# Moving the residual loads and the whole output stores from GpSimd's DMA queue to SyncE's

## The chip, the cores and the metric

The kernel runs on one core of one Trainium2 chip. The metric is device time in microseconds (us) of one execution, the median of several runs; lower is better. Engines are named as in the profile: PE is TensorE's matmuls, PEld its weight loads, DVE is VectorE, ACT is ScalarE, POOL is GpSimd, SP is SyncE. A "q" behind an engine's name (SPq, POOLq) means its instruction queue: instructions that set up, wait, branch or issue a DMA and do no arithmetic. Each queue takes its instructions strictly in order, so an instruction that waits holds all that stand behind it on the same engine.

## The reference

One layer over 2048 tokens of width 512, in bf16, is the sum of three terms: the residual x, a sliding-window attention of the normalized x, and a gated MLP of it that mixes tokens.

```python
def _A_ref(x, wqkv, wo):            # 32 heads of 16, window of 256 tokens
    ...
    p = _softmax(scores, axis=-1)
    o = jnp.einsum('bhqk,bhkd->bhqd', p, v)
    return (lambda x, *d: x.transpose(*d))(o, 0, 2, 1, 3).reshape(B, S, D) @ wo

def _B_ref(x, w_in, w_sp, b_sp, w_out):
    z = _gelu(jnp.einsum('bsd,df->bsf', x, w_in))
    z1 = z[..., :Fh].copy()
    z2 = _layernorm(z[..., Fh:], axis=-1)
    g = jnp.einsum('ts,bsf->btf', w_sp, z2) + b_sp[None, :, None]
    return jnp.einsum('bsf,fd->bsd', z1 * g, w_out)
x = A_x
xn = _layernorm(x, axis=-1)
return x + _A_ref(xn, A_wqkv, A_wo) + _B_ref(xn, B_w_in, B_w_sp, B_b_sp, B_w_out)
```

## The kernel before

**First stage (to about 84 us).** x is loaded, normalized and transposed into xnT; `z_half` (L280) makes both halves of z with a GELU; part of the q, k and v projections (`qkv_unit`, L111 and L129) is mixed in. POOL computes the reciprocal square roots (L238).

**Second stage (from about 84 us to the end).** The tokens are 16 tiles of 128, numbered t, and for attention 8 pairs of tiles, numbered J. The order of the work on PE is written out by hand in the string `ORDER`: S is a group of attention scores, m a mask, p the product with v, n a normalization, and the letters q, g and f with a number are so many matmuls of the projections, of the token mixing and of the output. The units that matter here:

- `g_work(t, j)` (L426 to L448): 16 matmuls of w_sp's transposed tile wspT(t) with z2, for half j of the columns; DVE then multiplies with z1 into u (L439). After the second half SP issues the transpose uT(t) of u by DMA (L446), and right behind it the load of wspT(t+2), also a DMA transpose (L414). There are two buffers of wspT.
- `f_work(t, c0)` (L462 to L487): 6 matmuls with uT(t) and 4 with the attention's transposed result, into one bank; DVE adds the residual tile xo(t) in place (L481), and the sum is stored from xo(t) to the output, out(t) (L487). Tile 15 is done in two halves of 256 columns, whose stores, out(15a) and out(15b), go out from SP and ACT.
- `load_xo(t)` (L452): the residual tile, 128 KB, into one of four buffers. Tiles 0 and 1 are asked for ahead of the second stage, and tile t+2 at the head of `f_work(t)`.
- `load_half(J)` (L403): two DMAs on SP (L406, L408) that copy parts of v into vh for pair J.
- `check_sums` (L628), called between DVE's addition of tile 13 and out(13): DVE checks the attention sums in three instructions, and SP sends the result `low` as one row by DMA (`row`, L639). At the end DVE reduces that row to a flag (L823, L826), all five engines load the flag (L829) and branch on it (L834): a second version of the attention runs if a sum was out of bounds, and is skipped here.

Behind the branch stands the end of the program (under L859 in the profile): SP waits for every DMA's and every engine's counter, each engine drains, and all meet at a barrier which POOL gathers and releases; then POOL clears the counters and all meet once more.

No scheduler moves instructions: each engine runs what the program records for it, in the order of recording. DMA completions are counted on eight counters for DMAs issued by SP and ACT, in turn, and on eight others for those of POOL.

Of the kernel before, what the change touches and what calls it, by code (L numbers as in the profile page):

```python
# [8 lines left out]
P = 128  # L9
# [6 lines left out]
D = 512  # L16
# [37 lines left out]
def kernel(  # L54
# [12 lines left out]
    nc = tc.nc  # L67
    x2 = A_x.flatten_outer_dims()
# [74 lines left out]
    with ExitStack() as actx:  # L143
# [20 lines left out]
        for half in range(2):  # L164
            for k, eng in ((0, nc.sync), (1, nc.scalar)):
# [3 lines left out]
                    out=w_in_sb[:, :, f0 : f0 + HALF], in_=w_in_v[:, :, f0 : f0 + HALF]  # L169
# [5 lines left out]
        with nc.allow_non_contiguous_dma(reason="tiny bias gather"):  # L175
# [3 lines left out]
            out=w_out_sb[:, 0:5, :], in_=B_w_out[0:640, :].rearrange("(c p) n -> p c n", p=P)  # L179
# [5 lines left out]
        for _ in range(WARM):  # L185
# [7 lines left out]
            out=hmask[:],  # L193
            in_=ident[:].rearrange("p (s e d) -> p e s d", s=4, e=2),
# [16 lines left out]
        for m, off in ((maskY, 0), (maskD, -PAD)):  # L211
            nc.gpsimd.memset(m[:], 1.0)
            nc.gpsimd.affine_select(
                out=m[:, 0:PAD], in_=m[:, 0:PAD], pattern=[[-1, PAD]],
# [3 lines left out]
                out=m[:, PAD:P], in_=m[:, PAD:P], pattern=[[1, PAD]],  # L218
# [231 lines left out]
    xos = {}  # L450

    def load_xo(t):  # L452
        xos[t] = cp.tile([P, D], BF, name="xo", bufs=4)
        nc.gpsimd.dma_start(out=xos[t][:], in_=x2[t * P : (t + 1) * P, :])

    for t in range(2):
        load_xo(t)

    def f_cols(t):
        return D // 2 if t == NB - 1 else D  # L460

    def f_work(t, c0):  # L462
        if c0 == 0 and t + 2 < NB:
            load_xo(t + 2)
        xo = xos[t]
        w = f_cols(t)
        fo = ps_x.tile([P, 512], F32, name="fo", tag="f")
        for ch in range(NFC):
            nc.tensor.matmul(  # L469
                fo[:, 0:w], lhsT=uTs[t][:, ch, :], rhs=w_out_sb[:, ch, c0 : c0 + w],  # L470
                start=(ch == 0), stop=False,
            )
            yield
        q0 = (1 - t % 2) * P
        for c in range(NC):
            nc.tensor.matmul(  # L476
                fo[:, 0:w], lhsT=oTs[t // 2][:, c, q0 : q0 + P], rhs=wo_sb[:, c, c0 : c0 + w],
                start=False, stop=(c == NC - 1),
            )
            yield  # L480
        nc.vector.tensor_tensor(  # L481
            out=xo[:, c0 : c0 + w], in0=fo[:, 0:w], in1=xo[:, c0 : c0 + w], op=ALU.add
        )
        if t == NB - 3:
            check_sums()
        eng = (nc.sync if c0 == 0 else nc.scalar) if w < D else nc.gpsimd
        eng.dma_start(out=out2[t * P : (t + 1) * P, c0 : c0 + w], in_=xo[:, c0 : c0 + w])  # L487

    E = {}
# [138 lines left out]
    def check_sums():  # L628
        assert not (later or units)
        r = r_all[:].rearrange("p a b -> p (a b)")  # L630
        ok = ep.tile([P, 512], BF, name="ok", tag="E")
        low = ep.tile([P, 1], F32, name="low", tag="E")
        nc.vector.tensor_scalar(out=ok[:], in0=r, scalar1=R_LOW, scalar2=None, op0=ALU.is_ge)
        nc.vector.scalar_tensor_tensor(
            out=ok[:], in0=r, scalar=R_HIGH, in1=ok[:], op0=ALU.is_le, op1=ALU.mult
        )
        nc.vector.tensor_reduce(out=low[:], in_=ok[:], axis=mybir.AxisListType.X, op=ALU.min)
        row = ep.tile([P, P], F32, name="row", tag="E")
        nc.sync.dma_start(out=row[0:1, :], in_=low[:])  # L639
        rows.append(row)  # L640


    def attention_with_maximum(gctx):
# [153 lines left out]
        "q": [(4, q_work(b, i)) for b, i in qkv_list],  # L797
        "g": [(NB, g_work(t, j)) for t in range(NB) for j in range(2)],
        "f": [(NFC + NC, f_work(t, c0)) for t in range(NB) for c0 in range(0, D, f_cols(t))],
    }  # L800
    left = 0
    for step in ORDER.split():
# [21 lines left out]
        out=low[0:1, :], in_=rows[0][0:1, :], axis=mybir.AxisListType.X, op=ALU.min  # L824
    )
    nc.vector.tensor_scalar(  # L826
        out=flag[0:1, :], in0=low[0:1, :], scalar1=0.5, scalar2=None, op0=ALU.is_lt
# [36 lines left out]
```

## Time and profile before

| what | value |
|---|---|
| runs of the kernel | 261.93, 262.01, 262.93 us, median 262.01 |
| span of the profiled execution, first to last instruction | 259.3 us |
| median less that span (what lies around it) | 2.7 us |
| PE busy | 250.8 us, 97% of the span |
| DVE, ACT, POOL busy | 205.2, 196.3, 36.9 us (79%, 76%, 14%) |
| granted TensorE clock | 0.999 |
| DMA | 25.86 MB, mean 100 GB/s |
| loads of xo by POOL | 16, of 128 KB, 2.4 us from issue to landing in the median |
| whole stores by POOL | 15, of 128 KB, 2.6 us in the same count |

The profiled execution has no other time of its own than its span; the three runs are other executions. The profile's page gives busy time by engine, a strip of 40 slices, the DMA queues, the chain of work that ended last, and the costliest groups of instructions. Views of the trace behind it list who waited for whom, the instructions of one line of the kernel (with the shortest, median and longest duration in nanoseconds), and each engine's instructions in order of time.

### The profile page before, as it was taken

How to read it: one execution, taken by the hardware profiler on the slowest of the kernel's cores; microseconds unless marked ns; L12 is line 12 of the kernel's file. 1: busy time of each engine (PE TensorE's matmuls, PEld its weight loads, DVE VectorE, ACT ScalarE, POOL GpSimd, SP SyncE). 2: the span in 40 equal slices, each digit the busy share in tenths (PEclk: the TensorE clock that was granted, in tenths of full speed). 3: DMA queues.
4: the chain of work that ended last, by engine and by line, in shares of the span. 5: the costliest groups of instructions: out<-in, count | busy, mean ns of one | idle time of the engine just before them, and what ended most of it. 6: DMA issues, size and time to landing. Idle time of an engine off the chain costs nothing.

```text
span 259.3 us, 8817 instructions
## 1 busy us (share of the span) xinstructions
PE 250.8 (97%) x3857; PEld 142.4 (55%) x3877; DVE 205.2 (79%) x425; ACT 196.3 (76%) x236; POOL 36.9 (14%) x80
## 2 busy tenths in 40 slices
PE   8999999999999999999999999999999999999991
PEld 2665555555555455655664565455565565646651
DVE  4796997874656888598888788989899978858781
ACT  2777546446456899999999999999989986888300
POOL 4120312111011530101010110111011021010100
PEclk9999999999999999999999999999999999999999
DMA  7984021027300206585174537846056925751321
GB/s 220 370 227 161 0 43 40 0 52 124 70 0 4 63 19 142 134 155 116 44 100 123 134 64 140 130 111 132 27 89 153 147 76 118 119 125 44 72 53 48
DMA packets 61707, 25.86 MB, mean 100 GB/s; under 512 B 53648, under 2 KB 59200, under 8 KB 61664
## 3 DMA queue, kind: packets, MB, share of 16 engines
q1 hardware_dynamic: 58688, 20.15, 38.1%
q0 software_dynamic: 1488, 4.07, 4.8%
q10 hardware_dynamic: 1488, 1.03, 1.4%
q8 instruction: 31, 0.51, 0.8%
q14 instruction: 12, 0.10, 0.2%
HBM read 8.41 MB, written 2.10 MB: 41 GB/s over the span
## 4 chain that ended last, share of the span: by engine, by line
PE 95%; DVE 1%; DMA 1%; issue 1%; POOL 0%
PE gf L433 31%; PE zp L280 14%; PE S L558 10%; PE o L519 9%; PE fo L469 8%; PE pj_o L111 7%; PE fo L476 6%; PE pj_f L111 4%; PE pj_f L129 3%; PE pj_o L129 2%; DMA xt<-in_A_x_dram 1%; PE tp L270 1%; DVE stats L228 1%; POOL rs L238 0%; DVE xo L481 0%
## 5 line engine op out<-in xcount | busy, mean ns | idle before, releaser
L608 ACT ACTIVATE E<-S 128x1024 bf16<-128x1024 f32 (+1 forms) x128 | 117.5, 1007 | 8.3 <-PE S L558 8.0
L433 PE MATMUL gf<-z2n,wspT 128*128 128x344 bf16 x512 | 83.3, 310 | 0.0
L433 PEld LDWEIGHTS <-wspT 128*128 128x128 bf16 x512 | 46.6, 98 | 28.6 <-issue 5.5
L280 PE MATMUL zp<-w_in_sb,xnT 128*128 128x344 bf16 x256 | 41.8, 309 | 0.0
L611 DVE TENSOR_TENSOR E<-E,maskY 128x2048 bf16<-128x2048 bf16 (+2 forms) x36 | 37.9, 1058 | 2.5 <-ACT E L608 2.4
L280 PEld LDWEIGHTS <-xnT 128*128 128x128 bf16 x256 | 24.8, 98 | 15.2
L583 ACT ACTIVATE ED<-S 128x1024 bf16<-128x1024 f32 x32 | 31.0, 1023 | 2.3 <-PE S L558 2.3
L558 PE MATMUL S<-qpad,kT 32*64 32x128 bf16 (+1 forms) x1008 | 32.6, 246 | 0.2
L526 DVE STREAM_TRANSPOSE ot<-o 128x512 f32<-128x512 f32 x32 | 22.3, 716 | 7.9 <-PE o L519 7.8
L487 POOL DMA_DIRECT2D out_dram<-xo x15 | 8.2, 546 | 120.7 <-DVE xo L481 111.5
L558 PEld LDWEIGHTS <-kT 32*64 32x64 bf16 (+1 forms) x1008 | 12.2, 98 | 22.3 <-issue 21.3
L469 PE MATMUL fo<-w_out_sb,uT 128*128 128x512 bf16 (+1 forms) x90 | 23.3, 366 | 0.9 <-issue 0.5
L439 DVE SCALAR_TENSOR_TENSOR u<-gf,b_all,z 128x344 bf16<-128x344 f32 x32 | 18.2, 568 | 7.3 <-PE gf L433 6.8
L519 PE MATMUL o<-E,v_y 128*32 128x128 bf16 (+1 forms) x736 | 23.1, 239 | 0.0
L238 POOL TENSOR_TENSOR rs<-ve,mhalf 128x2 f32<-128x2 f32 (+1 forms) x17 | 11.7, 690 | 69.4 <-DVE ve L235 69.4
L519 PE MATMUL o<-ED,vh 128*32 128x64 bf16 x960 | 21.1, 193 | 0.0
L287 ACT ACTIVATE z<-zp 128x688 bf16<-128x688 f32 x16 | 11.9, 744 | 11.0 <-PE zp L280 11.0
L111 PE MATMUL pj_o<-xnT,wqkv 128*128 128x512 bf16 x77 | 20.1, 379 | 0.2
L287 ACT ACTIVATE z2n<-zp 128x688 bf16<-128x688 f32 x16 | 11.9, 744 | 10.3 <-PE zp L280 10.3
L111 PEld LDWEIGHTS <-wqkv 128*128 128x128 bf16 x128 | 12.5, 98 | 12.6
L611 DVE TENSOR_TENSOR ED<-ED,maskC 128x2048 bf16<-128x2048 bf16 x16 | 19.4, 1210 | 0.0
L122 DVE TENSOR_SCALAR qpad<-qt,hmask 128x512 bf16<-128x512 bf16 x32 | 9.7, 346 | 11.8 <-ACT qt L120 11.8
(70 smaller groups left out, 264.8 us busy)
## 6 DMA issues: line engine op xcount, KB each, us to landing
vh<-v_y SPq DMA_DIRECT2D x15, 140.0 KB, 3.5
xo<-in_A_x_dram POOLq DMA_DIRECT2D x16, 128.0 KB, 2.4
out_dram<-xo POOLq DMA_DIRECT2D x15, 128.0 KB, 2.6
xt<-in_A_x_dram SPq DMA_DIRECT2D x3, 512.0 KB, 10.3
wqkv<-in_A_wqkv_dram SPq DMA_DIRECT2D x1, 1536.0 KB, 10.9
w_in_sb<-in_B_w_in_dram ACTq DMA_DIRECT2D x2, 344.0 KB, 5.7
w_in_sb<-in_B_w_in_dram SPq DMA_DIRECT2D x2, 344.0 KB, 6.2
w_out_sb<-in_B_w_out_dram SPq DMA_DIRECT2D x1, 640.0 KB, 6.0
```

Of the source, the lines that this page charges most:

```text
L111: nc.tensor.matmul(pt[:], lhsT=wqkv[:, c, w0 : w0 + P], rhs=xnT[:, c, t0 : t0 + 512], start=(c == 0), stop=(c == NC - 1),)
L280: nc.tensor.matmul(zp[:, j, 0:HALF], lhsT=xnT[:, c, PAD + n * P : PAD + (n + 1) * P], rhs=w_in_sb[:, c, f0 : f0 + HALF], start=(c == 0), s ...
L287: nc.scalar.activation(out=dst.rearrange("p (j f) -> p j f", j=2), in_=zp[:, :, 0:HALF], func=ACT.Gelu_apprx_tanh,)
L433: nc.tensor.matmul(gf[:, 0:HALF], lhsT=wspT[t][:, c, :], rhs=z2n[:, c, j * HALF : (j + 1) * HALF], start=(c == 0), stop=(c == NB - 1),)
L439: nc.vector.scalar_tensor_tensor(out=u[:, j * HALF : (j + 1) * HALF], in0=gf[:, 0:HALF], scalar=b_all[:, t : t + 1], in1=z1[:, t, j * HALF ...
L469: nc.tensor.matmul(fo[:, 0:w], lhsT=uTs[t][:, ch, :], rhs=w_out_sb[:, ch, c0 : c0 + w], start=(ch == 0), stop=False,)
L519: nc.tensor.matmul(o[32 * s : 32 * s + 32, c0 + r0 : c0 + r0 + n], lhsT=v[:, m, h * VW : h * VW + 32], rhs=rhs(s), start=(i == 0), stop=(i ...
L526: nc.vector.transpose(out=ot[:].rearrange("p b j -> p (b j)"), in_=o[:])
L558: nc.tensor.matmul(out, lhsT=kT[32 * s : 32 * s + 32, g, k0 : k0 + nk], rhs=qpad[J // 2][32 * s : 32 * s + 32, g, :, qs - q00 : qs - q00 + ...
L583: nc.scalar.activation(out=Ed[:, 16 * i : 16 * i + 16, :], in_=S[i][:].rearrange("p b (x q) -> p (b x) q", q=PAD), func=ACT.Exp, scale=SM_ ...
L608: nc.scalar.activation(out=o, in_=w, func=ACT.Exp, scale=SM_SCALE)
L611: nc.vector.tensor_tensor(out=out, in0=in0, in1=mask.unsqueeze(1).to_broadcast([P, in0.shape[1], in0.shape[2]]), op=ALU.mult,)
```

## The change

All loads of the residual (L454) and the fifteen whole stores of the output (L487) are issued by SP in place of POOL. The two half stores of tile 15 stay on SP and ACT.

```diff
     def load_xo(t):
         xos[t] = cp.tile([P, D], BF, name="xo", bufs=4)
-        nc.gpsimd.dma_start(out=xos[t][:], in_=x2[t * P : (t + 1) * P, :])
+        nc.sync.dma_start(out=xos[t][:], in_=x2[t * P : (t + 1) * P, :])
...
         if t == NB - 3:
             check_sums()
-        eng = (nc.sync if c0 == 0 else nc.scalar) if w < D else nc.gpsimd
+        eng = nc.scalar if c0 > 0 else nc.sync
         eng.dma_start(out=out2[t * P : (t + 1) * P, c0 : c0 + w], in_=xo[:, c0 : c0 + w])
```

The built programs show the same instructions in the same order on PE, DVE and ACT. POOL loses 31 instructions that issue a DMA and is left with memsets in the second stage; SP gains the 31. On SP they stand where the program records them: the load xo(t+2) at the head of `f_work(t)` and the store out(t) at its end, among the transposes, the loads of wspT and the copies into vh. The end of SP's work reads, in the order of the changed program: uT(14), xo(14), out(12), uT(15), xo(15), row, out(13), out(14), out(15a), load of the flag. At the end of the program SP's list of waits is eight long instead of twelve, since POOL's eight DMA counters (two in a wait) are gone.

## The prediction

> **What bounds the kernel now.** First I read the page's busy times and its chain of work that ended last.
>
> ```profile
> span 259.3 us, 8817 instructions
> PE 250.8 (97%) x3857; PEld 142.4 (55%) x3877; DVE 205.2 (79%) x425; ACT 196.3 (76%) x236; POOL 36.9 (14%) x80
> PE 95%; DVE 1%; DMA 1%; issue 1%; POOL 0%
> ```
>
> PE is the bound: busy for 97% of the span, 95% of the chain. In PE's instructions in order of time, the gaps from 88 to 254 us add up to under 1 us. So what the change touches can win nothing inside the second stage; it can only lose there, by delivering something late. What it could win lies where PE is idle: before about 6 us, where POOL issues no DMA, and after PE's last matmul, which ends at 253.9.
>
> Next, who waited for whom, for SP and POOL (columns: total wait in us, times, longest):
>
> ```profile
> SPq L446 <- DVE u L439: 95.0, 16, 11.5
> POOL out_dram L487 <- DVE xo L481: 111.5, 14, 14.9
> ```
>
> Both queues mostly wait for DVE: POOL to store xo, SP to transpose u. The 31 moved issues have room on SP if no wait holds what stands behind it.
>
> Third, the end. These are POOL's and SP's own instructions under L859, from 255.85 to 258.5 us and then from 258.5 on (count, shortest/median/longest in ns, first and last start):
>
> ```profile
> L859 POOLq DRAIN  x1: 2597/2597/2597, 255.9 to 255.9; - x1
> ```
>
> ```profile
> L859 SPq EVENT_SEMAPHORE  x12: 28/28/28, 256.1 to 256.8; - x12
> L859 SPq DRAIN  x2: 7/10/13, 256.8 to 256.9; - x2
> ```
>
> ```profile
> L859 POOLq EVENT_SEMAPHORE  x4: 17/17/17, 258.5 to 259.2; - x4
> L859 POOLq DRAIN  x2: 44/76/107, 258.7 to 259.0; - x2
> ```
>
> POOL stands in one DRAIN from 255.9 to 255.9 + 2.6 = 258.5. SP, the slowest of the others, is through its waits at 256.9. Only at 258.5 does POOL gather the barrier, and 0.8 us later the span ends. So the last wait of this program is POOL's DRAIN, 1.6 us longer than anything else needs. It is no wait for data: POOL's last store was issued at 252.91 and landed 2.0 us later, at 254.9, before the DRAIN began.
>
> **The change, part by part.** (xo(t), out(t), uT(t), wspT(t) are the DMAs of tile t; vh(J) the two of pair J.)
>
> *POOL without DMAs.* Its 31 issues of 0.55 us (17 us) go. They lay in POOL's waits and on no path of PE: 0.
>
> *The DRAIN.* What does it cost on a POOL that issued no DMA? The trace before can't show that. Its other POOL DRAINs bound it: 0.04 and 0.11 us right after the long one, 0.18 us at 0.4 us behind four memsets. The upper end is the 2.6 us itself. I take 0.1 us, the nearest rows: in the long one POOL had no arithmetic left (its last memset is at 242.1), and unfinished business of its DMA queue is what sets it apart from the short ones. The Trainium skill (VectorE: DVE Perf Modes, The DRAIN you can't avoid) gives the boilerplate DRAINs of all five engines as constant at about 12 ns. The 7 to 13 ns of SP's agree, the 2597 ns does not, so by that page it isn't boilerplate alone; with 12 ns in place of 0.1 us the sum would be the same, because SP then comes last.
>
> *What is late next.* SP. Its twelve waits take 0.7 us from 256.1 to 256.8, 0.06 us each. The changed program has eight, as POOL's DMA counters are gone: 4 x 0.06 = 0.25 us less. SP's last drain moves from 256.9 to 256.65, POOL gathers at 256.7 in place of 258.5: a gain of **1.8 us**. If the DRAIN stays at 2.6 us, the gain is 0.
>
> *31 more issues on SP, and who stands behind their waits.* An issue of a plain DMA on SP takes 0.39 (64 KB) to 0.58 us (128 KB): about 31 x 0.5 = 15 us, beside 95 us of waits on u alone. The danger is a store that waits for DVE's addition with a transpose behind it. I set the time at which POOL issued each store (its tile summed by then) against SP's issue of the next transpose: out(0) 122.2 before uT(4) 130.5; out(3) 151.26 before uT(6) 153.72; out(7) 187.73 before uT(9) 190.25; out(8) 198.12 before uT(10) 200.58; out(10) 211.1 before uT(11) 215.4; out(11) 231.6 before uT(14) 238.7; out(12) 241.6 before uT(15) 247.15. The smallest margin is 2.46 us, more than four issues of 0.58. Stores hold no transpose up: 0. The Trainium skill (DMA: Bandwidth & Descriptors, Anatomy of one DMA — SWDGE (gpsimd) path) says that any wait for a semaphore is held on the issuing sequencer. That speaks against the change, and by these margins it costs nothing until the end.
>
> *Loads of wspT.* They are needed soon. Issue plus time to landing, against PE's first matmul on it: wspT(2) 101.25 against 102.45, wspT(3) 109.2 against 110.6, wspT(13) 216.69 + 4.4 = 221.1 against 222.27, wspT(14) 223.54 + 5.8 = 229.3 against 230.2. Ahead of the first two SP gains only xo(0) and xo(1), at 84 to 86 us, where it is idle. Ahead of wspT(13), out(10) (ready at 211.1) now pushes the pair vh(7) from 205.1 to about 211.7; vh took 3.0 to 5.4 us to land, so it may be in flight until 217. wspT took 4.3 to 6.9 us: the cost is between 0 and 6.9 - 5.6 = 1.3 us. I take 0, the row itself (4.4 us), since vh is all but landed by then. Ahead of wspT(14) nothing is added.
>
> *xo(15).* It was issued on POOL at 242.23. On SP it stands behind uT(15), which waits for u: that is issued at 247.15 for 1.76 us, so xo(15) goes at 248.97. DVE needs it at 252.80, and may take it up to 253.5 without delaying the last addition (253.96 less 0.42 us of work). It must land within 4.5 us. xo took 2.4 us in the median on POOL's queue, SP's first 128 KB loads 4.1, the longest xo or store 5.0. Cost between 0 and 0.5 us; I take 0, by the 2.4 us.
>
> *Stores at the end.* out(13) was issued at 250.53. On SP it stands behind row, which waits for DVE's check until 252.10 and takes 0.52. Then out(13) at 252.7, out(14) at 253.3, out(15a) at 253.9, done at 254.3, ahead of the load of the flag at 254.76. A landing of 1.9 to 2.6 us brings out(15a) home by 255.8 to 256.5; SP's waits for the counters run from 256.1 to 256.6. Cost 0 to 0.3; I take 0.
>
> **Sum.** 259.3 - 1.8 = 257.5 us of span. Around the span lie 262.01 - 259.3 = 2.7 us, which I leave as they are: **260.2 us**, 0.7% below the median. A difference under 0.5% (1.3 us) can't be told from none.
>
> **The rivals.**
>
> *1. The DRAIN stays.* If its 2.6 us come from something else (being POOL's first DRAIN after a long program), the barrier is gathered at 258.5 as before: 262.0 us. For it: nothing shows what POOL does in it, and POOL's DMAs had landed. Against it: three short DRAINs on the same engine. By the Trainium skill (DMA: Bandwidth & Descriptors, Issuing engines are not separate DMA queues) issuing from several engines only saves sequencer time; by that the result would be the same 262.0. The rows here have the 17 us of issue time in waits, which agrees, but that rule is silent on the DRAIN. Chance 0.20.
>
> *2. Slower: xo(15) comes late.* One mechanism: on one queue, xo(15) stands behind a transpose that waits for the last u. Every us that it takes beyond 4.5 to land delays the last additions, the flag and the branch by as much. From 4.5 + 1.8 = 6.3 us on, the gain at the DRAIN is eaten. With the 6.9 us of the slowest wspT it is 260.2 + 2.4 = 262.6; with the 10.3 us of the x loads of the first stage, issued into full queues, 266.0. For it: the queue was slow whenever much stood in it. Against it: in the slice from 238 to 248 us the DMA engines are busy 0.21 of the time, and ahead of xo(15) stands only uT(15), which landed after 3.0 us. Chance 0.09.
>
> *3. Part is given back.* The DRAIN shrinks, but wspT(13) stalls PE by up to 1.3 us, or the last stores keep SP: 260.8 to 261.8 us. Chance 0.07.
>
> That the change doesn't do what it says is ruled out by the changed program: POOL issues no DMA there.
>
> **How the numbers follow.** The forecast has 0.64. Faster by over 0.5% means below 260.7: nearly all of the forecast, 0.62. Slower by over 0.5% means above 263.3: most of rival 2, with what I have not seen, 0.09. The rest is the same: rival 1, rival 3 and the edges, 0.29. Around the forecast the bounds reach from 0.6 us below (POOL's steps behind the barrier, two DRAINs of 0.107 and 0.044 us and a clearing of counters of 0.178, are 0.3 us that may shorten with fewer counters, and the runs of before differ by 0.1 us at the least and more) to 0.5 above. To leave out no more than 2 in 10 the range must take in rivals 3 and 1: 259.6 to 262.4 us. The forecast's own range is 259.6 to 260.7.
>
> **What would show it.** Right: POOL's DRAIN at 255.9 falls to about 0.1 us, its first EVENT_SEMAPHORE under L859 stands at 256.7, SP has eight waits there, and PE's last matmul still ends at 253.9. Step by step: SP's uT issues stand at the times above; PE shows no idle time before gf at 222.3; xo(15) lands before 252.8; DVE's last addition begins at 253.96. Wrong: a DRAIN of 2 us or more without DMAs (rival 1); the additions of tile 15 released by a DMA (rival 2); new gaps on PE before gf or fo (rival 3).

## The result, and the profile after

The changed kernel takes 259.92 us in the median of 6 runs (259.21 to 260.23), the kernel before, run beside it, 261.97 (6 runs, 261.42 to 262.93). The ratio is 0.9914, with a 95% interval of 0.9893 to 0.9935: faster by 0.9%. The forecast was 260.2.

The page after, first the same three lines as were shown of before:

```profile
span 258.2 us, 8833 instructions
PE 252.7 (98%) x3877; PEld 142.4 (55%) x3877; DVE 205.1 (79%) x425; ACT 196.5 (76%) x236; POOL 20.2 (8%) x49
PE 96%; DVE 1%; DMA 1%; issue 0%; POOL 0%
```

PE bounds the kernel as before. (Its busy time can't be compared here: the page after has 20 matmul records more.) POOL's 17 us of DMA issues are gone (36.9 to 20.2 us). The end of the program shows where the time went. POOL's and SP's instructions under L859 up to 257.4 us, and POOL's from there on (count, shortest/median/longest in ns, first and last start):

```profile
L859 POOLq DRAIN  x1: 41/41/41, 256.3 to 256.3; - x1
```

```profile
L859 SPq EVENT_SEMAPHORE  x8: 28/28/28, 256.9 to 257.3; - x8
L859 SPq DRAIN  x1: 13/13/13, 257.4 to 257.4; - x1
```

```profile
L859 POOLq EVENT_SEMAPHORE  x4: 17/17/17, 257.5 to 258.1; - x4
L859 POOLq DRAIN  x2: 34/58/82, 257.6 to 257.9; - x2
L859 POOLq EVENT_SEMAPHORE_RANGE_CLEAR  x1: 135/135/135, 257.7 to 257.7; - x1
```

The DRAIN of 2597 ns is one of 41 ns. POOL now waits for SP: SP's eight waits end at 257.4, POOL gathers at 257.46. To compare two executions here, count from the load of the flag (L829), since PE's work ended 0.75 us later in this one. Before, it began at 254.76, the gather came 3.77 us later and the end 4.55 us later; after, it began at 255.52, with the gather 1.94 and the end 2.64 us later. The end has become shorter by 1.91 us.

SP's queue from 84 us on (total wait, times, longest) shows that the 31 issues went into its waits:

```profile
SPq L446 <- DVE u L439: 60.5, 16, 8.6
SPq L487 <- DVE xo L481: 18.6, 6, 6.7
```

SP waits for u 60.5 us in place of 95.0, still 16 times: each transpose of u still waits for its data and not for a store.

### The profile page after: what moved, and what is told of

Same layout as the page of the kernel before. It is cut to its first block, busy times and chain, and to the rows that moved or that the text cites. A ratio compares the mean times of both kernels' runs of the same rounds, so it can differ in the third digit from the quotient of the medians.

```text
span 258.2 us, 8833 instructions
## 1 busy us (share of the span) xinstructions
PE 252.7 (98%) x3877; PEld 142.4 (55%) x3877; DVE 205.1 (79%) x425; ACT 196.5 (76%) x236; POOL 20.2 (8%) x49
## 4 chain that ended last, share of the span: by engine, by line
PE 96%; DVE 1%; DMA 1%; issue 0%; POOL 0%
PE gf L433 31%; PE zp L280 15%; PE S L558 11%; PE o L519 9%; PE fo L469 9%; PE pj_o L111 7%; PE fo L476 6%; PE pj_f L111 4%; PE pj_f L129 3%; PE pj_o L129 2%; DMA xt<-in_A_x_dram 1%; PE tp L270 1%; DVE stats L228 1%; POOL rs L238 0%; DVE xo L481 0%
## 5 line engine op out<-in xcount | busy, mean ns | idle before, releaser
L469 PE MATMUL fo<-w_out_sb,uT 128*128 128x512 bf16 (+1 forms) x102 | 24.6, 368 | 0.0
L476 PE MATMUL fo<-wo_sb,oT 128*128 128x512 bf16 (+1 forms) x68 | 17.7, 368 | 0.0
L519 PEld LDWEIGHTS <-v_y 128*32 128x32 bf16 x736 | 15.2, 97 | 4.0 <-issue 3.6
```

Source lines behind the costliest of these rows:

```text
L469: nc.tensor.matmul(fo[:, 0:w], lhsT=uTs[t][:, ch, :], rhs=w_out_sb[:, ch, c0 : c0 + w], start=(ch == 0), stop=False,)
L476: nc.tensor.matmul(fo[:, 0:w], lhsT=oTs[t // 2][:, c, q0 : q0 + P], rhs=wo_sb[:, c, c0 : c0 + w], start=False, stop=(c == NC - 1),)
L519: nc.tensor.matmul(o[32 * s : 32 * s + 32, c0 + r0 : c0 + r0 + n], lhsT=v[:, m, h * VW : h * VW + 32], rhs=rhs(s), start=(i == 0), stop=(i ...
```

## The experiments

**The kernel before, again.** No edit.

> The kernel before, unchanged: 262.0 us as before, and a span for each of its runs, which the first runs of before did not have. The median fell by 2.05 us, the spans of the two profiled executions by only 1.1 (259.3 to 258.2). In the runs of the changed kernel 1.7 us lie around the span. Theory A (all of the gain is in the span): the runs of before have 1.7 us around it too, and spans of about 260.3, so the profiled one was a quick one. Theory B (part of the gain is outside the span): 2.7 us lie around it here, and spans are about 259.3. Its profile should show POOL's 2.6 us DRAIN again, and whether PE's two short gaps of the profile after (0.44 us at 125, 0.34 us at 165) come and go by themselves.

It took 261.73 us (ratio 0.9991, 0.9975 to 1.0008). Theory A holds: 1.73 us lie around its span (median of 12 runs), 1.76 around those of 17 runs of before beside it, whose spans go from 259.4 to 261.2 with a median of 260.2. The profiled execution of before, with 259.3, was a quick one. Its own time must have been near 261.0. This second profile has the DRAIN of 2597 ns again, and the flag's load, gather and end stand as in the first (3.77 and 4.56 us). What differs is PE, here at 164 us of the span:

```profile
164.56 0.39 PE L558 MATMUL S<-qpad,kT 32*128 32x256 bf16 x5
165.45 0.29 PE L558 MATMUL S<-qpad,kT 32*128 32x256 bf16 x3 [0.49 <-issue]
```

PE stands for half a microsecond in the middle of a group of eight matmuls, released by nothing that the trace shows. The two short gaps of the profile after are of this kind. The one near 165 us is thus not of the change's making. The one near 125 us stands, 0.5 us long, also in the kernel before with a DRAIN added (below).

**The changed kernel, again.** No edit.

> The changed kernel once more: 259.9 us, 1.7 us around the span, POOL's DRAIN under 0.1 us. Does PE show the two short gaps (0.44 us at 125, 0.34 us at 165) again? If they belong to the change, they stand at the same places and the last matmul ends near 254.7; if they come by chance, it ends nearer to 253.9.

259.94 us (0.9916, 0.9892 to 0.9941), a DRAIN of 41 ns, gather and end 1.94 and 2.64 us behind the flag's load: the end is the same to 0.01 us. PE's gaps are at 125 and 135 us this time, 0.55 us each, with none at 165.

**Only the loads on SP; only the stores on SP.** Each edit is against the kernel before.

```diff
-        nc.gpsimd.dma_start(out=xos[t][:], in_=x2[t * P : (t + 1) * P, :])
+        nc.sync.dma_start(out=xos[t][:], in_=x2[t * P : (t + 1) * P, :])
```

> Only the loads of x are on SP; POOL keeps its fifteen stores, the last at about 252.9. Fixed price (any DMA on POOL makes the long DRAIN): DRAIN 2.6 us, 262.0 us. Price by the number of DMAs (31 gave 2.6): 15 give about 1.25 us, which ends at 257.1, 0.3 us after SP: 260.4 us. Rival of the prediction (a load behind a transpose comes late): xo(15) is issued near 249 as in the changed kernel and lands by 252; no delay, or up to 0.5 us more.

```diff
-        eng = (nc.sync if c0 == 0 else nc.scalar) if w < D else nc.gpsimd
+        eng = nc.scalar if c0 > 0 else nc.sync
```

> Only the stores are on SP; POOL keeps its sixteen loads, the last at about 242, some 14 us before its DRAIN. Fixed price: DRAIN 2.6 us, 262.0 us. Price of a recent DMA (only one that has just landed makes POOL wait): DRAIN 0.1 us, 260.0 us. Price by number: 16 give about 1.35 us, 260.4 us.

260.11 us (0.9927, 0.9902 to 0.9952) and 260.18 us (0.9930, 0.9908 to 0.9952). POOL's three DRAINs under L859, first of the loads on SP, then of the stores on SP:

```profile
L859 POOLq DRAIN  x3: 40/107/1291, 256.1 to 258.3; - x3
```

```profile
L859 POOLq DRAIN  x3: 44/107/1372, 257.8 to 259.7; - x3
```

1291 ns with fifteen DMAs left on POOL, 1372 ns with sixteen: the price by number, to a few hundredths of a microsecond. A price paid once for using POOL's queue falls, and so does a price of a recent DMA: with only loads left on POOL, its last DMA is issued at 236.98 us, 20.8 us before the DRAIN.

The length of the DRAIN follows the number, but with fifteen DMAs it isn't what makes the end late. There the DRAIN begins 0.83 us behind the flag's load and is over at 2.12, and SP is through its waits at 2.15. POOL gathers only at 2.47 (the first start here, 257.7):

```profile
L859 POOLq EVENT_SEMAPHORE  x4: 17/17/17, 257.7 to 258.4; - x4
```

POOL is held for 0.3 us in between. The run with twelve stores, below, comes back to this hold.

**One DMA on POOL, early or late.** The first load of a residual tile, or out(14), on POOL in the changed kernel.

```diff
-        nc.sync.dma_start(out=xos[t][:], in_=x2[t * P : (t + 1) * P, :])
+        (nc.gpsimd if t == 0 else nc.sync).dma_start(
+            out=xos[t][:], in_=x2[t * P : (t + 1) * P, :]
+        )
```

> The changed kernel, but the very first load of a residual tile, at 84 us, goes by POOL: one DMA, 170 us before the end. Fixed price: DRAIN 2.6 us and 262.0 us, all of the gain lost through one DMA. Price by number or by recency: DRAIN 0.1 us, 259.9 us. If part of the gain is outside the span, this shows whether one DMA on POOL brings that part back as well.

```diff
-        eng = nc.scalar if c0 > 0 else nc.sync
+        eng = nc.scalar if c0 > 0 else (nc.gpsimd if t == NB - 2 else nc.sync)
```

> The changed kernel, but out(14) goes by POOL, near 253.7: one DMA, 2.6 us before POOL's DRAIN begins. Fixed price: DRAIN 2.6 us, 262.0 us. Price by number: DRAIN 0.1 us, 259.9 us. Price of a recent DMA: a DRAIN of up to 2.6 us here, and 0.1 us where the one DMA is early.

259.53 us (0.9901, 0.9879 to 0.9922) and 259.81 us (0.9929, 0.9902 to 0.9956). Both have a first DRAIN of 140 ns, whether the one DMA was issued 170 us or under 3 us before it (early, where the edit makes L859 L861, then late):

```profile
L861 POOLq DRAIN  x3: 40/93/140, 255.9 to 257.6; - x3
```

```profile
L859 POOLq DRAIN  x3: 40/93/140, 256.0 to 257.6; - x3
```

So the price has nothing to do with how lately the data landed. The DRAIN grows with the DMAs that POOL has issued. The run with the early DMA is 0.4 us quicker than the changed kernel although its end is 0.11 us longer (2.75 us behind the flag's load). That stays open; it is no more than PE's pauses differ by from one execution to the next.

**The load one unit later.** This puts the slow rival's mechanism to the test. Every load moves back by one unit, and xo(15) comes to stand behind a wait that ends late.

```diff
-    for t in range(2):
+    for t in range(1):
         load_xo(t)
...
-        if c0 == 0 and t + 2 < NB:
-            load_xo(t + 2)
+        if c0 == 0 and t + 1 < NB:
+            load_xo(t + 1)
```

> The changed kernel with each residual tile loaded one unit later, tile t+1 at the head of the output unit of tile t (and only tile 0 ahead of the second stage). xo(15) then stands on SP behind row, which waits for DVE's check until 252.9, and behind out(13): it is issued at about 254.1 in place of 249.2. The slow rival's mechanism: it lands at about 254.1 + 2.5 = 256.6, the addition of out(15a) waits from 253.55 to 256.6, that of out(15b) ends 2.4 us later, and so does the program: 262.3 us. If the loads were not on the path that sets the end: 259.9 us.

262.29 us (ratio to before 1.0015, 1.0000 to 1.0029), 2.4 us above the changed kernel, as worked out. SP's and DVE's instructions in order of time (start, duration, what; DVE's idle time and its releaser in brackets):

```profile
252.57 0.53 SPq L639 DMA_DIRECT2D row<-low  x1
253.15 0.58 SPq L487 DMA_DIRECT2D out_dram<-xo  x1
253.78 0.43 SPq L454 DMA_DIRECT2D xo<-in_A_x_dram  x1
```

```profile
252.33 0.68 DVE L481 TENSOR_TENSOR xo<-fo,xo 128x512 bf16<-128x512 f32 x1
256.27 0.76 DVE L481 TENSOR_TENSOR xo<-fo,xo 128x256 bf16<-128x256 f32 x2 [3.26 <-DMA xo<-in_A_x_dram]
```

The load of tile 15 is issued at 253.78, behind row and out(13), and DVE's addition waits 3.26 us for it. The DRAIN is at its 41 ns here: the whole gain of the change is given back by one load in the wrong place of SP's queue. It is the only load that DVE waits for.

**A DRAIN of its own, early.** The kernel before, all of its DMAs on POOL.

```diff
         if c0 == 0 and t + 2 < NB:
             load_xo(t + 2)
+            if t + 2 == NB - 1:
+                nc.gpsimd.drain()
```

> The kernel before, with all its DMAs on POOL, and one DRAIN more on POOL: right behind the load of xo(15), at about 242.8 us of the profile of before, where POOL then waits some 8 us for out(13). The DRAINs so far are 2.597, 1.372, 1.291, 0.140 and 0.041 us with 31, 16, 15, 1 and 0 DMAs on POOL: 0.06 us and 0.082 us for each DMA. Theory: a DRAIN pays for the DMAs since the last DRAIN. Then the new one takes 0.06 + 29 x 0.082 = 2.4 us in POOL's idle time, the last one 0.06 + 2 x 0.082 = 0.22 us, and the kernel takes about 260.0 us, the changed kernel's time with POOL's queue kept. Rival: the price is for all DMAs of the program, at the end: the last DRAIN stays at 2.6 us, 261.9 us.

260.58 us against 262.21 for before beside it (0.9921, 0.9901 to 0.9941): the theory holds. It is 0.6 us more than the 260.0 expected. Half of that is the end, which is 2.97 us behind the flag's load and not 2.64, mostly because SP keeps its twelve waits; the runs of before beside it were also 0.2 us slower than those above. POOL's added DRAIN, and its three at the end (the edit moves later lines of the kernel down by two, so L859 is L861 here):

```profile
L466 POOLq DRAIN  x1: 3618/3618/3618, 243.6 to 243.6; - x1
```

```profile
L861 POOLq DRAIN  x3: 50/107/217, 257.3 to 258.8; - x3
```

The last one pays for two DMAs only, 217 ns. The early one takes 3.6 us in place of the 2.4 worked out. It was put down while the load ahead of it was still being issued (0.55 us), which leaves 0.6 us without an explanation. It lies in POOL's idle time and costs nothing.

**Twelve loads, six loads, twelve stores on POOL.** The changed kernel with part of one kind put back.

```diff
-        nc.sync.dma_start(out=xos[t][:], in_=x2[t * P : (t + 1) * P, :])
+        (nc.gpsimd if t < 12 else nc.sync).dma_start(
+            out=xos[t][:], in_=x2[t * P : (t + 1) * P, :]
+        )
```

> The changed kernel with the first twelve loads of x back on POOL. By 0.06 + 12 x 0.082 us POOL's DRAIN takes 1.04 us. In the changed kernel POOL has 1.1 us between the start of its DRAIN and the moment at which SP is through its waits, and here SP has up to four waits more (0.25 us). So the price is paid beside SP: 259.9 us, as with none. If each DMA on POOL cost its 0.082 us on the path of the end, it would be 260.9 us.

260.70 us (0.9938, 0.9919 to 0.9956): between the two. The DRAIN of 1046 ns is hidden as worked out: the gather is 2.17 us behind the flag's load, SP being through its waits at 2.15. But the end is at 3.40, not 2.95: POOL begins its second DRAIN 0.3 us late and takes 241 ns for it.

> The changed kernel with the first six loads of x back on POOL. With twelve, the barrier was gathered 2.17 us after the load of the flag, as a price of 1.04 us beside SP's waits asks (1.94 without POOL's DMAs, and 0.23 for SP's four more waits), but the profile showed POOL 0.45 us late behind the barrier, and the runs 260.7 us. Theory (the price is hidden; those 0.45 us have another cause): the DRAIN takes 0.06 + 6 x 0.082 = 0.55 us, the gather is at 2.12 to 2.17, the end at 2.95 after the load of the flag, 260.2 us. Rival (each DMA on POOL costs 0.08 us on the path of the end): 260.4 us with the gather near 2.4.

With `t < 6` in the same place: 260.24 us (0.9935, 0.9914 to 0.9956), a DRAIN of 556 ns, gather at 2.12, end at 2.90: the price is hidden.

```diff
-        eng = nc.scalar if c0 > 0 else nc.sync
+        eng = nc.scalar if c0 > 0 else (nc.gpsimd if t < 12 else nc.sync)
```

> The changed kernel with the first twelve stores on POOL in place of the loads: the same number of DMAs as with twelve loads, in other places of POOL's instruction stream. The DRAIN takes 1.04 us either way. If POOL's 0.45 us behind the barrier came with the number of its DMAs, they stand here too and the kernel takes 260.7 us; if they came with the place of its instructions or by chance, the end is at 2.95 after the load of the flag and the kernel takes 260.2 us.

260.37 us (0.9935, 0.9916 to 0.9955), a DRAIN of 1046 ns to the digit, gather at 2.18, second DRAIN at its usual place with 107 ns, but the end at 3.26. So POOL is late behind the barrier with twelve loads and with twelve stores, at different instructions.

A hold of about 0.3 us stands once in the end of every kernel here whose POOL issues twelve DMAs or more, and in none with six or fewer. With sixteen and with all 31 it lies right behind the branch: the first DRAIN there begins 1.11 to 1.17 us behind the flag's load, in the others at 0.83. With fifteen it lies between the DRAIN and the gather, with twelve behind the barrier. With twelve and fifteen it comes ahead of the same one of POOL's recorded instructions, the 115th of the program; the kernels without the hold record only 99 to 107. So it goes with the place in POOL's instruction stream. What causes it stays open. In the kernel before it delays the DRAIN itself, so by these starts about 0.3 us of the gain come from the hold and not from the DRAIN's length.

The first DRAINs at the end of all the kernels, over the number of DMAs that POOL had issued since the last one:

| DMAs on POOL | 0 | 1 | 2 | 6 | 12 | 15 | 16 | 31 |
|---|---|---|---|---|---|---|---|---|
| DRAIN, us | 0.041 | 0.140 | 0.217 | 0.556 | 1.046 | 1.291 | 1.372 | 2.597 |

From 1 to 31 DMAs this is 0.058 us and 0.082 us for each, to 0.01 us, for loads and stores alike. Each of these DMAs is 128 KB, so the runs don't tell a price by number from one by bytes. The early DRAIN (29 DMAs, 3.618 us) is not in the table and lies 1.2 us above the line.

## Why the prediction was right, point by point

**PE's second stage wins nothing.** Right: in the profile after PE has no gap ahead of gf or fo. Its gaps are the ones that come and go from one execution to the next. By them the last matmul ends at 254.67 and not, as the text had it as a sign, at 253.9.

**The DRAIN, 0.1 us on a POOL without DMAs.** Right: 0.041. The reason given, unfinished business of POOL's DMA queue, was right in kind and said too little. That business grows with each DMA. The prediction had one number to go by, and could not have told 0.082 us for each of 31 from 2.6 us once; the runs with 15, 16, 12, 6, 2 and 1 DMAs do. The twelve and six on POOL also show that the price costs nothing as long as it is shorter than SP's way to the barrier. With POOL's counters in its list SP is through at 2.15: that leaves 1.3 us from a DRAIN that begins at 0.83, some fifteen DMAs, and 1.0 us from one that begins at 1.13 as before, some eleven.

**What is late next: SP, with four waits less.** Right: it is through at 1.92 us behind the flag's load in place of 2.15, 0.23 against 0.25. The step from 3.77 to 1.94 us at the gather is 1.83 us; the forecast was 1.8. It was read from the end of the DRAIN, so it held POOL's 0.3 us ahead of the DRAIN without naming them. Not priced was what lies behind the gather: 0.78 us before, 0.70 after, since POOL's second and third DRAIN and its clearing of the counters became shorter (0.107, 0.044 and 0.178 us to 0.082, 0.034 and 0.135). The text had this in the range and not in the sum.

**Stores hold no transpose up.** Right: the smallest margin was 2.46 us for uT(6) and uT(10), and SP issues these at 154.15 and 201.33, the 0.4 and 0.75 us later by which PE is later there.

**wspT(13), between 0 and 1.3 us, taken as 0.** Right. vh(7) is issued at 212.02 in place of 205.13 (211.7 was worked out) and lands 4 us later; wspT(13) takes 4.4 us as before. (vh's shortest landing was 2.35 us, not 3.0; nothing hangs on that.)

**xo(15).** Right: issued at 249.20 behind uT(15), landed 2.5 us later, at 251.7. DVE's addition at 253.55 is released by PE. The last lines of DVE's work after:

```profile
253.55 0.42 DVE L481 TENSOR_TENSOR xo<-fo,xo 128x256 bf16<-128x256 f32 x1 [0.18 <-PE fo L476]
254.71 0.42 DVE L481 TENSOR_TENSOR xo<-fo,xo 128x256 bf16<-128x256 f32 x1 [0.74 <-PE fo L476]
255.35 0.14 DVE L826 TENSOR_SCALAR flag<-low 1x1 int32<-1x1 f32 x1
```

The rival's price for lateness was sound, as the load one unit later shows: there it costs 2.4 us. What kept it away is 1.8 us of slack on this one load.

**Stores at the end.** Right: out(13), out(14) and out(15a) are issued behind row from 253.51 to 255.06, ahead of SP's load of the flag at 255.52, and SP's waits for the counters run through without a stop.

**The time around the span, 2.7 us.** This term was wrong. It is 1.7 to 1.8 us in the runs of both kernels. The 2.7 came from setting the median of three runs against the span of a fourth execution, which was a quick one by 0.9 us. It did no harm because the same amount was taken off and put on again. The sum that the runs bear out is 261.97 - 1.91 = 260.06 us; measured are 259.92 and 259.94. The rest, 0.1 us, is less than the runs differ by.

**Rival 1, the DRAIN stays, is refuted.** The Trainium skill (DMA: Bandwidth & Descriptors, Issuing engines are not separate DMA queues) says that issuing on several engines only saves the sequencer's time. Here each DMA of 128 KB issued by POOL also costs 0.082 us at POOL's next DRAIN, so the measurement decides against the rule's "only". The same skill's 12 ns for boilerplate DRAINs (VectorE: DVE Perf Modes, The DRAIN you can't avoid) fits SP (7 to 13 ns) and is off for POOL even without any DMA (41 ns), if the DRAINs under L859 are of that kind, which no run shows.

What the DRAIN does for each DMA was not seen. That it grows with them and doesn't depend on direction or age was: loads and stores have one price, and an early DMA has that of a late one. Their size was never varied.

## What to carry to other kernels

Read the end of a profile under the last line of the program, engine by engine: the longest DRAIN there may be the last wait of the whole kernel, though no share of busy time shows it. DMAs issued by GpSimd leave a bill there, here 0.082 us for each of 128 KB, which is free while another engine is still on its way to the barrier, and can be paid early by a DRAIN in GpSimd's idle time where its queue is wanted. When DMAs move to one in-order queue, look for the one that then stands behind the latest wait; here a load one unit later gave the whole gain back.

## What the runs showed of the hardware

PE pauses at four fixed places of its instruction stream (at 125, 135, 164 and 183 us), each time for 0 to 0.8 us, with POOL's DMAs and without, and not in every execution; in the profiles taken these pauses add up to between about 0.1 and 2.0 us. The places lie multiples of 128 weight loads apart to within one (257, 640 and 383), each load with its matmul, and the page's instruction queue moves 31 packets, 0.51 MB. That these are late loads of instructions is a guess that no run tried. Between the two profiles of the kernel before they make 0.7 of the 1.05 us by which the spans differ. That they are also most of why its spans go from 259.4 to 261.2 us is likely and not shown. This spread is why a single profile against a median gave a wrong time around the span.
